# Attention followed by a gated MLP on one core: steps of VectorE and ScalarE in another order, low terms last, short scores read straight through

## The chip, the core and the metric

The kernel runs on one core of a Trainium2 chip. A time is the device time of one execution in microseconds (us), from the first to the last instruction and a little around it. Five engines work side by side, each through its own instructions in order: TensorE (PE, with its weight loads listed apart as PEld), VectorE (DVE), ScalarE (ACT), GpSimd (POOL) and SyncE (SP), which issues nearly all DMAs.

## The reference

```
scores = q @ k^T / sqrt(64) - log(448)          # 8 batches x 12 heads, 448 tokens, head size 64
x      = sigmoid(scores) @ v                    # heads side by side: 448 x 768
h      = relu(x @ w_in)                         # 768 -> 1024
u, v2  = h[:, :512], h[:, 512:]
v_n    = (v2 - mean(v2)) / sqrt(var(v2) + 1e-6) # over the 512 features
v_s    = w_spatial @ v_n + b_spatial            # over the 448 tokens
out    = (u * v_s) @ w_out                      # 512 -> 768
```

All inputs and the output are fp32.

## The kernel before, in words

**Number format.** Most products are made from pairs: a value is rounded to fp32r (the high part), what is lost is kept as a second fp32r (the low part), and three products are added in PSUM: high by high, low by high, high by low (`TERMS`, line 347). So each operand costs a rounding copy (mostly on ScalarE) and a subtraction (on VectorE) before TensorE can use it. A few products run in plain fp32 without a split: the short scores (line 373) and attention times v (lines 440 and 1462).

**Rounds.** The batches are taken in four rounds of two (`m` = 0 to 3). A round has these stages, one after the other on TensorE:

- attention, heads in groups of four. 448 tokens of keys are three full tiles of 128 and a short one of 64. The short tiles of two head pairs share one call of `score_products` with `t == NFULL`: four matmuls on 64 x 64 quarters of the array, in two passes each, so eight matmul records. There are six such calls in a round. Every score product reads the queries through `halves`, which turns the order (t s) into (s t): consecutive columns lie half a row apart. ScalarE applies the sigmoid out of PSUM (`sigmoid`, line 355).
- the v half of the MLP's input: in round 0 plain products and the layer norm by `gate_values`, in rounds 1 to 3 `values_by_blocks`;
- the u half: in round 0 `gated`, in rounds 1 to 3 the first part of `gated_by_blocks`;
- the product over tokens, `spatial` (line 1012), four groups of two PSUM banks, of which the token tiles are the result of the layer norm (`vns`);
- the output product, `output_by_blocks`.

**Seven products for eight.** The block stages (line 1078, `by_blocks`) multiply a 2 x 2 grid of blocks with seven block products. They need sums of operands, made at run time by VectorE: from the four gated blocks (g11, g12, g21, g22) come t1 to t4, each of which has to be rounded (`high`, ScalarE, line 1159) and subtracted (`low`, VectorE, line 1163). The order of the blocks is fixed (`ORDER_1`, `ORDER_V`). The results are accumulated in banks px, pw and py; between blocks ScalarE copies them out (lines 735, 1239, 1325, 1336) and VectorE adds them (lines 738, 1246, 1337, 1353), and a bank can take its next block only after that. Two such banks share one tile.

**What sets the order.** Each engine runs its instructions in program order (`in_program_order`), so the place of a step in the source is its place in the queue. Steps that are not needed at once are generators in `jobs`; `spare(n)` runs the next n pieces of them, and is called from `then` after each block's bank. `rest` (in `values_by_blocks`), `steps` (in `by_tokens`, the layer norm of rounds 1 to 3) and `first_rest` (the sums and splits of the gated blocks) are such jobs. `load_weights(n)` runs n pieces of another generator, which in round 0 decodes and splits the weights w_in and w_out (two pieces for a weight tile, on VectorE and ScalarE, lines 157 to 163 and 252 to 289); `load_weights(99)` before the third `gated` runs all that is left. `high_of_sum` and `low_of_sum` (lines 626 and 630) split the sums of w_out in round 0, and the second sends the result out by a DMA on SP.

In `gate_values` of round 0, ScalarE applies the relu, VectorE the statistics, GpSimd the power of -1/2, and VectorE subtracts the mean (line 799), scales (line 810) and makes the low part (line 811). In `by_tokens`, ScalarE already does the subtraction and the scaling (lines 909 and 911).

Of the kernel before, what the change touches and what calls it, by code (L numbers as in the profile page):

```python
# [35 lines left out]
def attn_gmlp_kernel(  # L36
# [319 lines left out]

    def copied(b, hp, t):
        return t == NFULL - 2
# [7 lines left out]
    def score_products(b, hp, t):  # L366
        psc = banks(f"psc_{b}_{hp}_{t}")
        if t == NFULL:
            for odd in range(2):
                raw = loaded[b, hp + odd]  # L370
                for j in range(2):
# [4 lines left out]
                        halves(raw[rows, HALF + Q :]),  # L376
# [42 lines left out]
    def attention_scores(b, hp, t):  # L419
        psc = score_products(b, hp, t)  # L420
        at = room(b, hp, t)
        if copied(b, hp, t):
            nc.vector.tensor_copy(at, psc)
            subtract_lows()
        else:
            sigmoid(at, psc)
# [221 lines left out]
    def values_by_blocks(m):  # L648
# [24 lines left out]
        def high(name, src):  # L673
            if name == "t1":
                nc.scalar.copy(x1[0], src)
            else:
                for ks, t in to[name]:
# [12 lines left out]
        high("t3", w3)  # L690
# [3 lines left out]
        low("t3", w3)  # L694

        def rest():
            high("t2", w00)
# [72 lines left out]
    def gate_values(ts):  # L770
# [14 lines left out]
        if n > 1:  # L785
            load_weights(1 if ts[0] else 5)
# [10 lines left out]
        nc.gpsimd.tensor_tensor(rstd[:, :n], rstd[:, :n], mhalf[:, :n], op=ALU.pow)  # L797
        for i in range(n):
            nc.vector.tensor_scalar_sub(rv[:, i], rv[:, i], mv[:, i, 0:1])
        load_weights(n - 1)  # L800
        for i, t in enumerate(ts):
            vn = slots["tile"][:, t]
            if t != NFULL:
                parts = [(vn[:, 0], vn[:, 1], slice(0, P))]
            else:

                a, c = slice(0, HALF), slice(HALF, P)
                parts = [(vn[a, 0], vn[c, 0], a), (vn[c, 1], vn[a, 1], c)]
            for hi, lo, rows in parts:
                nc.vector.tensor_scalar_mul(hi, rv[rows, i], rstd[rows, i : i + 1])  # L810
                nc.vector.scalar_tensor_tensor(
                    lo,
                    rv[rows, i],
                    rstd[rows, i : i + 1],
                    hi.bitcast(F32),
                    op0=ALU.mult,
                    op1=ALU.subtract,
                )
            vns[t] = vn
        if n == 1:  # L820
            load_weights(1)

    def by_tokens(m):
# [107 lines left out]
        def steps():  # L931
# [9 lines left out]
            moments(a)  # L941
            relu(b)
            yield True
            relu(c)
# [12 lines left out]
            yield True  # L957
            moments(b)
            yield True
# [38 lines left out]
    def spatial(b, fcs):  # L998
# [3 lines left out]
        for i, fc in enumerate(fcs):  # L1002
            fs = slice(fc * P, (fc + 1) * P)
            ops = [
                (vns[c + 4 if b % 2 else c][:, a, fs], w_sp_s[:, c, p, cols])
# [747 lines left out]
```

## Time and profile before

| | |
|---|---|
| median of 3 runs | 624.38 us (622.73 to 627.30) |
| the profiled execution's own time | 624.51 us |
| its span, first to last instruction | 622.5 us |
| mean granted clock of TensorE in it | 0.999 of full speed |
| busy: PE, PEld | 612.6 us (98%), 487.1 us (78%) |
| busy: DVE, ACT, POOL | 453.4 us (73%), 341.0 us (55%), 21.4 us (3%) |
| DMA | 139.22 MB, 224 GB/s mean |

How to read it: a matmul's record lasts longer than the time until the next one can start, because matmuls are pipelined. So a PE that is busy for 98% is not a PE without waits, and the weight loads (PEld), of which there is one for each matmul, show the waits better: in a stage of 128 x 128 tiles they stand back to back when nothing is late. In the attention stages four loads of 64 x 64 run side by side and PEld is idle most of the time without any wait.

### The profile page before, as it was taken

How to read it: one execution, taken by the hardware profiler on the slowest of the kernel's cores; microseconds unless marked ns; L12 is line 12 of the kernel's file. 1: busy time of each engine (PE TensorE's matmuls, PEld its weight loads, DVE VectorE, ACT ScalarE, POOL GpSimd, SP SyncE). 2: the span in 40 equal slices, each digit the busy share in tenths (PEclk: the TensorE clock that was granted, in tenths of full speed). 3: DMA queues.
4: the chain of work that ended last, by engine and by line, in shares of the span. 5: the costliest groups of instructions: out<-in, count | busy, mean ns of one | idle time of the engine just before them, and what ended most of it. 6: DMA issues, size and time to landing. Idle time of an engine off the chain costs nothing.

```text
span 622.5 us, 10390 instructions
## 1 busy us (share of the span) xinstructions
PE 612.6 (98%) x4136; PEld 487.1 (78%) x4136; DVE 453.4 (73%) x639; ACT 341.0 (55%) x444; POOL 21.4 (3%) x63
## 2 busy tenths in 40 slices
PE   9999999998999999999999999999999999999997
PEld 3556689997856669999984568998996655999996
DVE  4898798999789878278785657628788555935873
ACT  6889313235488863272556785137347766515443
POOL 0000011000000000020000000002000000002000
PEclk9999999999999999999999999999999999999999
DMA  8774853369987879890695652597169554559145
GB/s 291 261 232 143 258 148 105 118 236 325 319 341 282 324 285 327 245 412 11 202 317 204 231 233 102 137 297 300 51 218 368 182 179 189 160 142 380 63 150 179
DMA packets 59632, 139.22 MB, mean 224 GB/s; under 512 B 15680, under 2 KB 31552, under 8 KB 59328
## 3 DMA queue, kind: packets, MB, share of 16 engines
q1 hardware_dynamic: 59152, 138.22, 64.3%
q8 instruction: 32, 0.52, 0.4%
q10 hardware_dynamic: 432, 0.34, 0.2%
q14 instruction: 16, 0.13, 0.1%
HBM read 102.37 MB, written 36.18 MB: 223 GB/s over the span
## 4 chain that ended last, share of the span: by engine, by line
PE 65%; DVE 19%; ACT 8%; DMA 3%; issue 3%; SPq 0%; POOL 0%; ACTq 0%; DVEq 0%
PE pav L1462 14%; PE psc L391 13%; PE vx L1078 7%; PE pg L1012 5%; PE pav L440 5%; PE ux L1078 4%; PE o L1078 4%; PE psc L373 4%; PE vy L1078 3%; PE uy L1078 3%; DVE x_s L1163 3%; ACT x_s L1159 2%; ACT ats L355 1%; PE pv L473 1%; DVE wval_s L160 1%
## 5 line engine op out<-in xcount | busy, mean ns | idle before, releaser
L355 ACT ACTIVATE ats<-psc,fixed 128x896 f32<-128x896 f32 x102 | 95.0, 1015 | 18.0 <-PE pav L1462 10.1
L391 PEld LDWEIGHTS psc<-qks 64*128 64x128 f32 x840 | 77.3, 187 | 14.9 <-issue 7.2
L391 PE MATMUL psc<-qks 64*128 64x448 f32 x840 | 85.4, 359 | 0.0
L1462 PE MATMUL pav<-ats,v 64*64 64x448 f32 x720 | 76.4, 540 | 0.0
L1078 PE MATMUL o<-x_s,w_out 128*128 128x448 f32 x324 | 65.0, 356 | 0.9
L1078 PEld LDWEIGHTS o<-x_s,w_out 128*128 128x128 f32 x324 | 60.0, 189 | 4.9 <-DVE vr L1337 2.6
L1012 PE MATMUL pg<-w_sp_s,mlp 128*128 128x448 f32 x320 | 63.3, 355 | 0.5 <-DVE mlp L916 0.3
L1012 PEld LDWEIGHTS pg<-w_sp_s,mlp 128*128 128x128 f32 x320 | 59.6, 189 | 3.3 <-DVE mlp L916 1.8
L1462 PEld LDWEIGHTS pav<-ats,v 64*64 64x64 f32 x720 | 28.4, 132 | 38.5 <-issue 26.6
L341 DVE TENSOR_TENSOR qks<-raw,qks 128x848 fp32r<-128x848 f32 x46 | 47.3, 1038 | 1.0
L1078 PE MATMUL vx<-x_s,w_g 128*128 128x448 f32 x216 | 43.0, 355 | 0.8 <-ACT vr L735 0.8
L1078 PEld LDWEIGHTS vx<-x_s,w_g 128*128 128x128 f32 x216 | 40.3, 189 | 4.0 <-issue 2.1
L1078 PE MATMUL ux<-x_s,w_u 128*128 128x448 f32 x162 | 32.1, 352 | 0.0
L1078 PEld LDWEIGHTS ux<-x_s,w_u 128*128 128x128 f32 x162 | 30.6, 189 | 0.0
L473 PE MATMUL pv<-w_g_s,x_s 128*128 128x512 f32 x126 | 28.9, 390 | 0.0
L473 PEld LDWEIGHTS pv<-w_g_s,x_s 128*128 128x128 f32 x126 | 23.6, 188 | 5.6 <-PE pav L440 0.7
L473 PE MATMUL pu<-x_s,w_u_s 128*128 128x448 f32 x144 | 27.4, 352 | 0.0
L473 PEld LDWEIGHTS pu<-x_s,w_u_s 128*128 128x128 f32 x144 | 27.2, 189 | 0.0
L440 PE MATMUL pav<-ats,v 128*64 128x448 f32 (+1 forms) x144 | 27.1, 544 | 0.0
L1462 PE MATMUL pav<-at,v 64*64 64x448 f32 x168 | 26.9, 536 | 0.0
L373 PE MATMUL psc<-raw 64*64 64x448 f32 x192 | 26.8, 637 | 0.0
L1246 DVE TENSOR_TENSOR us<-uy,us 128x448 f32<-128x448 f32 x6 | 3.7, 621 | 30.0 <-ACT us L1245 30.0
(205 smaller groups left out, 1003.7 us busy)
## 6 DMA issues: line engine op xcount, KB each, us to landing
raw<-qk_dram SPq DMA_DIRECT2D x47, 456.0 KB, 6.1
w_g<-w_g SPq DMA_DIRECT2D x21, 768.0 KB, 6.2
w_u<-w_u SPq DMA_DIRECT2D x21, 768.0 KB, 7.1
w_out<-w_out SPq DMA_DIRECT2D x21, 768.0 KB, 10.4
v<-v_dram SPq DMA_DIRECT2D x24, 448.0 KB, 4.2
wraw<-w_in_dram SPq DMA_DIRECT2D x12, 512.0 KB, 5.1
v<-vt SPq DMA_DIRECT2D x48, 112.0 KB, 2.6
wraw<-w_out_dram SPq DMA_DIRECT2D x6, 512.0 KB, 4.2
```

Of the source, the lines that this page charges most:

```text
L160: nc.vector.scalar_tensor_tensor(l, a, 3, l, op0=ALU.logical_shift_left, op1=ALU.bitwise_or)
L341: nc.vector.tensor_sub(s[:, 1], loaded[b, hp][:, HALF:], s[:, 0].bitcast(F32))
L355: nc.scalar.activation(at, src, AF.Sigmoid, bias=bias_s, scale=QK)
L373: nc.tensor.matmul(psc[odd * HALF : (odd + 1) * HALF, j, :S], raw[rows, :HALF], halves(raw[rows, HALF + Q :]), start=True, stop=True,)
L391: nc.tensor.matmul(psc[:, j, :S], st[rows, k : k + P], halves(mv[rows, Q:PART]), start=i == 0, stop=i == len(ops) - 1,)
L440: nc.tensor.matmul(pav[heads, odd, :S], vt[rows, t, heads], at[rows, j], start=start, stop=t == NFULL,)
L473: nc.tensor.matmul(ps, st, mv, start=i == 0, stop=i == len(ops) - 1)
L1012: nc.tensor.matmul(pg[:, i, :S], st, mv, start=n == 0 and not ended, stop=n == len(ops) - 1 and ended,)
L1078: nc.tensor.matmul(out_ps, stationary(w, i, k)[:, a], halves(moving[mv][k][c]), start=(to, i) not in started and n == 0, stop=n == len(ops ...
L1159: nc.scalar.copy(homes[name][0][:, i], src[:, i])
L1163: nc.vector.tensor_sub(lo[:, i], src[:, i], hi[:, i].bitcast(F32))
L1462: ins = nc.tensor.matmul(pavs[pair][heads, i % 2, :S], vt[rows, t if t == NFULL else t + i % 2 * (NFULL + 1), heads], at[rows, j], start=i ...
```

## The change

Six edits, without any change of what is multiplied:

- Short scores (`score_products`): the queries are read straight through, not by halves. The permutation is done by ScalarE instead, whose `short_sigmoid` writes the attention weights two elements apart.
- `gate_values` (round 0): ScalarE subtracts the mean and scales; VectorE negates the mean and keeps the low part. `load_weights` is called with other numbers at other places (12 pieces within the four calls of `gate_values`; before, 11).
- `values_by_blocks`: the second third of t3's rounding and t3's low part go from before the first block into the job `rest`, and the first bank of the first block calls `spare` too.
- `by_tokens`: the statistics (`moments`) of tile groups a and b come one call of `spare` later.
- `spatial` and `by_blocks`: the low terms come last (in `by_blocks`, last among those of a bank; in `spatial`, each bank's ten terms are cut in two parts, and the first part is done for both banks before the second).
- `gated_by_blocks` and `output_by_blocks`: `first_rest` becomes `later_parts`, in which the steps have other places; t1 is written over g12 instead of g22; in round 0 the splits of the sums of w_out move from `of_21` into it, and the low part of g21 into `of_22`; the add for t2 moves into `of_22` in rounds 1 to 3; the bank copies of t3 call `spare` too; and `rooms` takes its buffers in another order. One piece of `spare` in attention moves from the first group of four heads to the second.

```diff
+    def short_sigmoid(at, src):
+        sigmoid(
+            at.rearrange("p j (s t) -> p j t s", t=2),
+            src.rearrange("p j (t s) -> p j t s", t=2),
+        )
...
                         raw[rows, :HALF],
-                        halves(raw[rows, HALF + Q :]),
+                        raw[rows, HALF + Q :],
...
-        high("t3", w3)
+        high("t3", w3, 0)
         nc.vector.tensor_sub(xl[:, 1], pav[:, :, :S], xl[:, 0].bitcast(F32))
         nc.vector.tensor_sub(w01, w01, w00)
         nc.vector.tensor_add(w00, w3, w00)
-        low("t3", w3)
 
         def rest():
+            high("t3", w3, 1)
+            low("t3", w3)
+            yield True
             high("t2", w00)
...
             if mv == "11":
                 nc.scalar.copy(r1[:, i], px[i])
-                spare(i)
+                spare(1)
...
+        mean = scale[:, 1]
+        nc.vector.tensor_scalar_mul(mean[:, :n], mv[:, :n, 0], -1.0)
         for i in range(n):
-            nc.vector.tensor_scalar_sub(rv[:, i], rv[:, i], mv[:, i, 0:1])
-        load_weights(n - 1)
+            nc.scalar.activation(rv[:, i], rv[:, i], AF.Identity, bias=mean[:, i : i + 1])
...
+        for i, hi, _, rows in homes:
+            nc.scalar.activation(hi, rv[rows, i], AF.Identity, scale=rstd[rows, i : i + 1])
+        load_weights(steps[1])
+        for i, hi, lo, rows in homes:
+            nc.vector.scalar_tensor_tensor(
+                lo,
+                rv[rows, i],
...
             relu(a)
             yield True
+            relu(b)
+            yield True
             moments(a)
-            relu(b)
-            yield True
             relu(c)
...
             low_parts(d)
             yield True
+            yield True
             moments(b)
-            yield True
             highs(b)
...
+        highs, lows = ([(c, a, p) for c in range(NFULL) for p in range(2 - a)] for a in range(2))
+        short = [(NFULL, b % 2, 0)]
+        if b % 2:
+            terms = highs[:4] + lows[:2] + short + highs[4:] + lows[2:]
+        else:
+            terms = highs + lows + short
+        n = len(terms) // 2
+        for part in (terms[:n], terms[n:]):
+            for i, fc in enumerate(fcs):
+                for term in part:
...
-            ops = [(a, k, c) for k in range(nk) for a, c in TERMS]
+            ops = [(a, k, c) for part in (TERMS[:2], TERMS[2:]) for k in range(nk) for a, c in part]
...
+            def sub_t1():
+                nc.vector.tensor_sub(g12, g22, g11)
+
+            def sub_t4():
+                nc.vector.tensor_sub(r2, g21, g11)
...
+            if m:
+                steps = {
+                    1: (hi("t3"), lo("t3")),
+                    2: (hi("t2"),),
+                    4: (hi("22"), lo("t2")),
+                    5: (sub_t1, hi("t1"), sub_t4),
+                    6: (lo("t1"),),
+                    9: (lo("22"),),
+                    11: (hi("t4"),),
+                    14: (lo("t4"),),
+                }
+            else:
+                steps = {
+                    1: (low_sum("s3"),),
+                    2: (hi("t3"), lo("t3"), hi("22"), high_sum("s2")),
+                    5: (add_t2, hi("t2"), low_sum("s2"), lo("t2"), high_sum("s1")),
+                    6: (sub_t1, hi("t1"), sub_t4),
+                    7: (low_sum("s1"),),
+                    8: (lo("t1"),),
+                    9: (high_sum("s4"), low_sum("s4")),
+                    10: (lo("22"),),
+                    11: (hi("t4"),),
+                    14: (lo("t4"),),
+                }
+            for n in range(15):
+                for step in steps.get(n, ()):
+                    step()
+                yield True
...
         def of_21(pu):
             if not m:
                 high_of_sum("s3")
-                high_of_sum("s2")
             gate(g21, pu)
             high("21", g21)
-            if not m:
-                low_of_sum("s3")
-            low("21", g21)
-            if not m:
-                high_of_sum("s1")
-                high_of_sum("s4")
+            if m:
+                low("21", g21)
 
         def of_22(pu):
             gate(g22, pu)
+            if not m:
+                low("21", g21)
             nc.vector.tensor_sub(g12, g22, g12)
+            if m:
+                add_t2()
...
-                for name in ("c12", "r2", "thirds")
+                for name in ("r2", "c12", "thirds")
...
-            sigmoid(at, score_products(*units[n], NFULL))
+            short_sigmoid(at, score_products(*units[n], NFULL))
...
-                spare(8 if n + 4 == end else 4 if n > first else 5)
+                spare(8 if n + 4 == end else 5 if n > first else 4)
...
+                ((0, 1), (6, 1, 0)),
+                ((2, 3), (1, 1, 0)),
+                ((4, 5), (1, 1, 0)),
+                ((6,), (0, 0, 1)),
```

## Rows read from the trace of the kernel before

**Rows 1.** Windows: length, busy time (instructions) of five engines, clock, DMA share, GB/s.

```profile
66.90:100.00 33.10, 33.10 (x151) 27.71 (x151) 27.18 (x54) 10.21 (x15) 3.48 (x6) 1.00 0.58 174
...
317.70:377.30 59.60, 59.60 (x601) 34.84 (x602) 35.44 (x41) 44.00 (x48) 1.24 (x9) 1.00 0.62 228
```

**Rows 2.** Timeline of PEld, round 2: start, length, form, count, idle before and releaser.

```profile
377.17 3.32 PEld L1078 LDWEIGHTS vx<-x_s,w_g 128*128 128x128 f32 x18 [0.70 <-issue]
381.10 3.32 PEld L1078 LDWEIGHTS vx<-x_s,w_g 128*128 128x128 f32 x18 [0.61 <-ACT vr L735]
...
401.45 3.40 PEld L1078 LDWEIGHTS ux<-x_s,w_u 128*128 128x128 f32 x18
...
415.64 3.33 PEld L1078 LDWEIGHTS uy<-x_s,w_u 128*128 128x128 f32 x18 [0.57 <-DVE stats L886]
...
425.77 1.41 PEld L1012 LDWEIGHTS pg<-w_sp_s,mlp 128*128 128x128 f32 x7
427.79 0.30 PEld L1012 LDWEIGHTS pg<-w_sp_s,mlp 128*128 128x128 f32 x2 [0.60 <-DVE mlp L916]
428.57 2.00 PEld L1012 LDWEIGHTS pg<-w_sp_s,mlp 128*128 128x128 f32 x11 [0.48 <-DVE mlp L916]
...
443.65 6.83 PEld L1078 LDWEIGHTS o<-x_s,w_out 128*128 128x128 f32 x36
...
452.18 2.19 PEld L1078 LDWEIGHTS o<-x_s,w_out 128*128 128x128 f32 x12 [0.48 <-DVE vr L1353]
...
461.58 1.05 PEld L1078 LDWEIGHTS o<-x_s,w_out 128*128 128x128 f32 x6 [0.40 <-DVE vr L1337]
...
468.99 0.21 PEld L373 LDWEIGHTS psc<-raw 64*64 64x64 f32 x8 [0.28 <-issue]
```

**Rows 3.** Timeline of PEld, the output stage of round 0.

```profile
139.13 3.40 PEld L1078 LDWEIGHTS o<-mlp,w_out_s 128*128 128x128 f32 x18
144.24 1.05 PEld L1078 LDWEIGHTS o<-x_s,w_out_s 128*128 128x128 f32 x6 [1.70 <-ACT ur L1325]
...
166.74 0.21 PEld L373 LDWEIGHTS psc<-raw 64*64 64x64 f32 x8 [0.28 <-issue]
```

**Rows 4.** Timeline of all engines, the start of that stage.

```profile
140.12 1.15 DVE L1156 SCALAR_TENSOR_TENSOR g<-pu,g 128x448 f32<-128x448 f32 x2
...
142.20 1.56 ACT L626 CAST w_out_sums<-wt 128x768 fp32r<-128x768 f32 x2
...
143.66 0.52 ACT L1325 COPY ur<-o 128x448 f32<-128x448 f32 x1
```

**Rows 5.** Timeline of all engines, round 2.

```profile
379.21 1.41 ACT L678 CAST xs<-whole 128x896 fp32r<-128x896 f32 x2
...
450.51 1.08 DVE L1174 TENSOR_TENSOR g<-g,g 128x896 f32<-128x896 f32 x1
...
459.07 0.53 ACT L1330 COPY othirds<-o 128x448 f32<-128x448 f32 x1 [1.42 <-PE o L1078]
...
468.27 1.15 DVE L1350 TENSOR_TENSOR or<-o,or 128x448 f32<-128x448 f32 x2
```

**Rows 6.** Groups by line: tile, form, count, then busy us, mean ns, idle before.

```profile
L391 PE MATMUL psc<-qks 64*128 64x448 f32 x840 | 85.4, 359 | 0.0
...
L1462 PE MATMUL pav<-at,v 64*64 64x448 f32 x168 | 26.9, 536 | 0.0
L373 PE MATMUL psc<-raw 64*64 64x448 f32 x192 | 26.8, 637 | 0.0
...
L160 DVE SCALAR_TENSOR_TENSOR wval_s<-wraw,wval_s 128x512 uint32<-128x512 uint32 x18 | 12.4, 688 | 0.2
...
L909 ACT ACTIVATE rv<-rv,scale 128x512 f32<-128x512 f32 x15 | 10.1, 714 | 2.5 <-DVE scale L892 2.4
...
L253 ACT ACTIVATE wraw<-wraw 128x512 f32<-128x512 f32 x12 | 8.3, 692 | 19.1 <-DVE wraw L252 18.8
...
L810 DVE TENSOR_SCALAR mlp<-rv,scale 128x512 fp32r<-128x512 f32 (+1 forms) x8 | 3.8, 481 | 0.8 <-POOL scale L797 0.8
```

More of the change, by code (lines that the diff above doesn't have):

```diff
@@ L671, in values_by_blocks, with high @@
         }
-        def high(name, src):
+        def high(name, src, only=None):
             if name == "t1":
@@ L676, in high @@
             else:
-                for ks, t in to[name]:
+                for ks, t in to[name][only : None if only is None else only + 1]:
                     nc.scalar.copy(t[:, 0], src[:, ks])
@@ L1001, in spatial @@
         pg = pgs[b, fcs]
[L1002 to L1005, printed above, removed]
-                for c in range(NFULL)
-                for a, p in TERMS
-            ]
-            ops.append((vns[NFULL][:, b % 2, fs], w_sp_s[:, NFULL, 0, cols]))
-            ended = (b, fcs) in begun
-            for n, (st, mv) in enumerate(ops):
-                nc.tensor.matmul(
-                    pg[:, i, :S],
-                    st,
-                    mv,
-                    start=n == 0 and not ended,
-                    stop=n == len(ops) - 1 and ended,
-                )
+        ended = (b, fcs) in begun
+        highs, lows = ([(c, a, p) for c in range(NFULL) for p in range(2 - a)] for a in range(2))
[8 more added lines that the diff above has]
+                for term in part:
+                    c, a, p = term
+                    t = c + 4 if b % 2 and c < NFULL else c
+                    nc.tensor.matmul(
+                        pg[:, i, :S],
+                        vns[t][:, a, fc * P : (fc + 1) * P],
+                        w_sp_s[:, c, p, cols],
+                        start=term == terms[0] and not ended,
+                        stop=term == terms[-1] and ended,
+                    )
         begun.add((b, fcs))
@@ L1163, in low, with add_t2 @@
             nc.vector.tensor_sub(lo[:, i], src[:, i], hi[:, i].bitcast(F32))
-        def first_rest():
-            high("22", g22)
-            yield True
-            high("t3", g12)
-            if not m:
-                low_of_sum("s2")
-            low("t3", g12)
-            yield True
-            yield True
-            nc.vector.tensor_add(g11, g12, g11)
-            high("t2", g11)
-            yield True
-            yield True
-            low("t2", g11)
-            low("22", g22)
-            nc.vector.tensor_sub(g22, g22, g11)
-            high("t1", g22)
-            if not m:
-                low_of_sum("s1")
-            low("t1", g22)
-            yield True
-            nc.vector.tensor_sub(r2, g21, g11)
-            if not m:
-                low_of_sum("s4")
-            yield True
-            yield True
-            high("t4", r2)
-            yield True
-            low("t4", r2)
-            yield True
+        def add_t2():
+            nc.vector.tensor_add(g11, g12, g11)
@@ new lines, in later_parts, with hi, lo, high_sum @@
+        def later_parts():
+            sources = {"t3": g12, "t2": g11, "22": g22, "t1": g12, "t4": r2}
+            def sub_t1():
+                nc.vector.tensor_sub(g12, g22, g11)
+            def sub_t4():
+                nc.vector.tensor_sub(r2, g21, g11)
+            def hi(name):
+                return lambda: high(name, sources[name])
+            def lo(name):
+                return lambda: low(name, sources[name])
+            def high_sum(name):
+                return lambda: high_of_sum(name)
+            def low_sum(name):
+                return lambda: low_of_sum(name)
+            if m:
[26 more added lines that the diff above has]
+                yield True
@@ L1325, in then @@
                 nc.scalar.copy(r1[i], px[i])
+                spare(1)
+            elif mv == "t3":
                 spare(1)
```

49 lines of the change are left out of this document (22 added, 27 removed).

## The prediction, as it was put on record

> **What bounds the kernel now.** First the page's busy shares and the windows. In round 2's attention TensorE is busy for all of 59.60 us, ScalarE for 44.00 and VectorE for 35.44 [rows 1]: TensorE sets the pace there, and only cheaper matmuls can help. The block stages I read from the weight loads, because a matmul's record hides a wait. A load of 128 x 128 that nothing delays takes 6.83 / 36 = 0.19 us (more exactly 0.189, since the stalls repeat to the hundredth) [rows 2]. So 126 matmuls, which each of the three block stages of a round has, need 23.8 us. In round 2 the v half starts at 377.17, the u half at 401.45, the token product at 425.77, the output at 443.65 and the next attention at 468.99 [rows 2]. That makes 24.28, 24.32 and 25.34 us for the three stages (from the last I take the 0.28 us of its change of tile): losses of 0.45, 0.5 and 1.25 us. Rounds 1 and 3 show the same waits within 0.2 us. Round 0's output stage runs from 139.13 to 166.74 [rows 3]: 27.61 − 0.28 − 23.8 = 3.5 us lost. These losses, and the short scores, are what the change can reach; each wait names a copy or an add that stood behind other work in its queue.
>
> **The change, part by part**
>
> *Short scores.* All three products here have 448 columns. The fp32r one, read by halves, has records of 359 ns; the plain fp32 one of short scores, read by halves, 637; the plain fp32 one by v, read straight, 536 [rows 6]. The last two have the same tile shape and differ by 101 ns. There are 192 records, four side by side, so 48 passes: 48 × 0.101 = 4.8 us if the reading is the reason. The means hold stretched records too, so I take 0.093 a pass, 4.5 us. Ends: 0 (the two tiles differ in more than the stride) and 4.8. All but the first calls of a round lie on TensorE's path. ScalarE now writes two elements apart. The nearest row reads and writes two apart in place: 692 ns for 512 elements, against 714 for 512 plain ones [rows 6]. I take nothing; the upper end is a doubling, 1 us a call, six a round, against 59.6 − 44.0 = 15.6 us in which ScalarE is free [rows 1].
>
> *Round 0's layer norm.* VectorE loses 15 passes of about 481 ns, ScalarE gains 15 of 714 [rows 6], and four small negations come. By the Trainium skill, "ScalarE: Activation LUTs", Rules for kernel authors, such adds and multiplies belong on VectorE; the sum would then lose 15 × 0.23 = 3.5 us. The rows of the window say otherwise: ScalarE is busy for 10.21 of 33.10 us, VectorE for 27.18 [rows 1], so I put ScalarE's time at nothing. VectorE's saving is not worth 7 us either: its low parts now wait for GpSimd's power and ScalarE's copies, and by stepping the four groups forward the last low part ends where it did. What is left is one piece of weight work that moves into VectorE's idle time, two joins of 0.69 [rows 6]: everything queued on VectorE from there to the output stage comes 1.4 us earlier. SP's load of the next weight tile moves with it.
>
> *Round 0's output.* Before, VectorE reaches g21's gate at 140.12, ScalarE casts two sums of w_out at 142.20 and only then copies the first bank, 143.66 to 144.18 [rows 4], on which TensorE waits until 144.24 [rows 3]. After: gate at 138.7, rounded by 140.8; first bank's copy by 141.4, before TensorE wants the second block at 139.13 + 18 × 0.189 = 142.5. VectorE then does g22's gate, g21's low part and the difference (about 1.1 each) until 143.3, a sum's low part and t3's until 145.3, and the three adds by 146.9; TensorE wants the first of these banks at 145.9. The sums that follow stay ahead by a few tenths, except t1's low part, which I put 0.3 late. SP's write of the first sum falls behind the raw loads, of which no user is near. So 3.5 becomes about 0.4: **3.1 us**. Ends: 1.5 (VectorE not earlier) and 3.5.
>
> *Values, rounds 1 to 3.* ScalarE rounds t3 twice, 1.41 us, before the first bank's copy, and TensorE waits [rows 5, 2]. One rounding (about 0.47) now stands behind that copy: 0.45 becomes 0.1, times three **1.1**. t3's low part comes later, but low terms last give it 1.1 us.
>
> *u half.* The wait of 0.57 us is for an add behind the statistics of group a [rows 2]. They now follow it: 3 × 0.5 = **1.5**. The statistics are then 0.6 late for the token product, which wants them: next item.
>
> *Token product.* Round 2 waits 0.60 and 0.48 us for low parts [rows 2]. Low terms last gives those two microseconds, but the fifth term is now a high part of the third tile, which I find about 0.8 late there, for its data come by DMA. Rounds 1 and 3 hardly wait. **0.5** in all; ends −0.5 and 1.5.
>
> *Output, rounds 1 to 3.* The third block waits 0.48 us for an add behind t2's sum, 450.51 to 451.59; the copy of t2's third bank waits until 459.07 for a buffer, which delays the next copies, and the sixth block waits 0.40 and 0.48 [rows 2, 5]. The sum now stands before the stage, and the buffer is free early. New: a copy of the first block stands behind t3's rounding, 0.3, and t2's sum pushes the adds by 0.1. 1.25 becomes 0.4: **2.5**. Against it: before, the last add ends 469.42 (468.27 + 1.15) [rows 5], as TensorE is done. VectorE does as many passes as before, so a shorter output leaves its adds behind, and the next attention's second bank waits: −0.3 for each of three starts, with 0.1 of each faster short call lost: **−1.0**.
>
> The piece of `spare` that moves in attention, and the relus that move by a step, lie under TensorE's work; uncovered they would cost their 1 us each.
>
> Sum: 4.5 + 3.1 + 1.1 + 1.5 + 0.5 + 2.5 − 1.0 = 12.2 us. The profiled execution took 624.51 us, 0.13 over the median, so the sum goes on either: 624.5 − 12.2 = **612.3 us**.
>
> **Rivals**
>
> 1. *The short reads give nothing.* For: the fp32r product is read by halves as well and shows no penalty, 359 ns [rows 6]. Against: 637 and 536 for like tiles. The Trainium skill, "TensorE: Matmul & The Clock Gate", Part 2, Step-by-step, says of the fill that the time depends on the number of columns alone; by that rule the reading would be free either way. The two fp32 groups of the trace, with equal columns, disagree with it. Time: 612.3 + 4.5 = 616.8. Chance 0.12.
> 2. *VectorE becomes the bound round the output stages.* What the reordering takes out of the waits there comes back as waits for its adds and for the statistics, because its work is the same. For: it runs from 140 us on without a pause, and its last adds end with TensorE. Against: the waits of before come from order, not from load. If half of the non-short gains (7.7) go: 616.2. Chance 0.18.
> 3. *Slower: ScalarE's strided write.* Place: the short sigmoid of every call. Free time is 15.6 us a round [rows 1], six calls: past 2.6 us more per call, ScalarE would be the bound of the attention, and past about 3.3 it would eat the 12 us in three rounds. At 4 us more, 3 × (24 − 15.6) = 25 us against 12: 638. Nothing in the rows is near it. Chance 0.03.
> 4. *More than forecast.* All waits named go: 3.5 + 1.35 + 1.5 + 1.1 + 3.7 + 4.8 = 16.0, 608.5. Chance 0.09.
>
> **How the numbers follow.** The forecast holds 0.58. The range 608.0 to 618.0 takes in rivals 1, 2 and 4 with the ends of the terms, and leaves out the slower case and a mixture of 1 and 2 (620), together near 0.15. 1% is about what a measurement of this kernel can tell from no change; faster by more than that means under 618.1: 0.58 + 0.09 + most of 0.12 and 0.18, say 0.85. Within 1%: 0.12, where rivals 1 and 2 meet. Slower: 0.03.
>
> **What would show it.** Short scores: records near 540 ns, and attention stages about 1.1 us shorter in each round. Output of round 0: no load waiting more than 0.5 us, and g21's gate within a microsecond of the start of the stage. Rounds 1 to 3: v half and u half within 0.2 us of 23.8, no wait on line 1353 or 1337 over 0.2, and a new small one at the output's second block or at the next attention's start. Wrong would be: short records still at 630; the short sigmoid far over 1 us; new waits on VectorE that add up to more than 2 us a round.

## The result, and the profile after

The changed kernel takes 614.02 us (median of 613.41 to 615.16) against 624.65 for the kernel before on the same chip: a ratio of **0.983**, interval 0.981 to 0.985. That is 10.6 us less; forecast were 12.2 (612.3 us, range 608 to 618). The execution with a profile is the longest of its four, 615.16 us with a span of 613.4, so the stages below add up to 9.1 us, the difference of the two spans, and not to 10.6.

A stage is measured from the first weight load of one to that of the next, as in the prediction; the output of round 3, behind which nothing comes, to the end of its last weight load. Gains in us, rounds 1 to 3 together unless a round is named:

| Stage | before | after | gain | forecast |
|---|---|---|---|---|
| attention, four rounds (62.87, 59.85, 59.59, 59.37 before) | 241.68 | 237.17 | 4.5 | 4.5 − 1.0 |
| round 0, from its v half to the end of its u half | 72.35 | 72.29 | 0.1 | 0 |
| round 0, output | 27.61 | 24.62 | 3.0 | 3.1 |
| v half | 72.85 | 71.49 | 1.4 | 1.1 |
| u half | 73.16 | 73.09 | 0.1 | 1.5 |
| token product | 51.02 | 51.66 | −0.6 | 0.5 |
| output | 75.72 | 74.99 | 0.7 | 2.5 |

Both rows of round 0 and the v half came as forecast. The attention gave what was forecast for the short scores, without the −1.0; 0.8 of its 4.5 us lie in the first attention, which varies by a microsecond from kernel to kernel. The last three rows should have given 4.5 and gave 0.2.

Windows of the changed kernel, in answer to [rows 1]:

```profile
66.12:99.22 33.10, 33.10 (x152) 27.72 (x153) 25.06 (x49) 19.07 (x29) 3.36 (x6) 1.00 0.65 206
311.24:369.60 58.36, 58.36 (x601) 34.50 (x602) 36.28 (x42) 44.20 (x48) 1.26 (x9) 1.00 0.63 232
```

In round 0's layer norm ScalarE went from 10.21 to 19.07 us, VectorE from 27.18 to 25.06. Round 2's attention is 1.2 us shorter at the same work. Groups by line, in answer to [rows 6]:

```profile
L397 PE MATMUL psc<-qks 64*128 64x448 f32 x840 | 84.8, 356 | 0.0
...
L1500 PE MATMUL pav<-at,v 64*64 64x448 f32 x168 | 26.9, 536 | 0.0
...
L379 PE MATMUL psc<-raw 64*64 64x448 f32 x192 | 22.0, 543 | 0.0
...
L355 ACT ACTIVATE at<-psc,fixed 128x896 f32<-128x896 f32 x12 | 13.2, 1102 | 3.0 <-PE psc L379 3.0
```

The short score product is now as cheap as the product by v (543 against 536 ns; before, 637). The short sigmoid takes 1102 ns; the plain ones average 1017. Weight loads of round 0's output and round 2, in answer to [rows 3] and [rows 2]:

```profile
138.29 3.40 PEld L1093 LDWEIGHTS o<-mlp,w_out_s 128*128 128x128 f32 x18
141.69 3.40 PEld L1093 LDWEIGHTS o<-x_s,w_out_s 128*128 128x128 f32 x18
145.28 3.32 PEld L1093 LDWEIGHTS o<-x_s,w_out_sums 128*128 128x128 f32 x18 [0.18 <-ACT w_out_sums L634]
...
153.25 5.97 PEld L1093 LDWEIGHTS o<-mlp,w_out_sums 128*128 128x128 f32 x32 [0.49 <-DVE mlp L1178]
...
369.48 3.32 PEld L1093 LDWEIGHTS vx<-x_s,w_g 128*128 128x128 f32 x18 [0.70 <-issue]
372.96 3.32 PEld L1093 LDWEIGHTS vx<-x_s,w_g 128*128 128x128 f32 x18
...
393.31 3.40 PEld L1093 LDWEIGHTS ux<-x_s,w_u 128*128 128x128 f32 x18
...
407.88 3.32 PEld L1093 LDWEIGHTS uy<-x_s,w_u 128*128 128x128 f32 x18 [0.95 <-issue]
...
414.88 3.32 PEld L1093 LDWEIGHTS uy<-x,w_u 128*128 128x128 f32 x18 [0.27 <-DVE scale L904]
418.21 0.76 PEld L1027 LDWEIGHTS pg<-w_sp_s,mlp 128*128 128x128 f32 x4
419.76 2.95 PEld L1027 LDWEIGHTS pg<-w_sp_s,mlp 128*128 128x128 f32 x16 [0.80 <-ACT mlp L923]
...
426.81 0.30 PEld L1027 LDWEIGHTS pg<-w_sp_s,mlp 128*128 128x128 f32 x2 [0.42 <-ACT mlp L923]
427.60 8.62 PEld L1027 LDWEIGHTS pg<-w_sp_s,mlp 128*128 128x128 f32 x46 [0.49 <-DVE mlp L928]
...
436.22 5.67 PEld L1093 LDWEIGHTS o<-x_s,w_out 128*128 128x128 f32 x30
442.83 1.05 PEld L1093 LDWEIGHTS o<-x_s,w_out 128*128 128x128 f32 x6 [0.93 <-ACT wval_s L1361]
444.09 3.32 PEld L1093 LDWEIGHTS o<-x_s,w_out 128*128 128x128 f32 x18 [0.20 <-DVE vr L1391]
```

The wait of 1.70 us in round 0's output is gone, and so is that of 0.61 in the v half, now 23.83 us long in each round, which is 126 loads back to back. In the output of round 2 the waits of [rows 2] are gone too, but a new one of 0.93 stands at the second block, and the same in rounds 1 and 3 (0.94 each). The token product has new waits, 0.42 and 0.49, for the parts of tile group b; the 0.49 is there in every round. The wait of 0.80 at its fifth load in round 2 is the one that the prediction had put there.

All engines of the changed kernel, in answer to [rows 4] (the gate, then the copy of the first bank):

```profile
136.78 1.15 DVE L1171 SCALAR_TENSOR_TENSOR g<-pu,g 128x448 f32<-128x448 f32 x2
...
139.81 0.54 ACT L1361 COPY ur<-o 128x448 f32<-128x448 f32 x1 [0.85 <-PE o L1093]
...
144.25 0.82 ACT L634 CAST w_out_sums<-wt 128x768 fp32r<-128x768 f32 x1
```

and, in answer to [rows 5], VectorE and ScalarE round the start of round 2's output stage (436.22):

```profile
427.46 1.08 DVE L1048 TENSOR_TENSOR g<-pg,b_bc 128x896 f32<-128x896 f32 x1
...
430.68 1.09 DVE L1178 TENSOR_TENSOR x_s<-g,x_s 128x896 fp32r<-128x896 f32 x1 [1.00 <-ACT x_s L1174]
...
440.28 1.09 DVE L1253 TENSOR_TENSOR g<-wval_s,g 128x896 f32<-128x896 f32 x1
441.41 0.94 ACT L1174 CAST x_s<-g 128x896 fp32r<-128x896 f32 x1 [2.00 <-DVE g L1253]
442.25 0.53 ACT L1361 COPY wval_s<-o 128x448 f32<-128x448 f32 x1
```

This is the place to read slowly. The copy of the third bank (442.25) stands in ScalarE's queue behind the rounding of t3 (441.41), which waits for the difference on VectorE (440.28 to 441.37). TensorE wanted that bank at 436.22 + 30 × 0.189 = 441.89. The difference is the end of a chain of VectorE that begins with the bias of g11 at 427.46 and takes 13.9 us. So two remedies offer themselves: take the copy out from behind the rounding, or make the chain end earlier. The experiments try both.

### The profile page after: what moved, and what is told of

It reads as the page before. It is cut to its first block, busy times and chain, and to the rows that moved or that the text cites. A ratio compares the mean times of both kernels' runs of the same rounds, so it can differ in the third digit from the quotient of the medians.

```text
span 613.4 us, 10394 instructions
## 1 busy us (share of the span) xinstructions
PE 604.1 (98%) x4136; PEld 486.3 (79%) x4136; DVE 447.5 (73%) x628; ACT 353.0 (58%) x459; POOL 24.3 (4%) x63
## 4 chain that ended last, share of the span: by engine, by line
PE 75%; DVE 9%; ACT 8%; DMA 3%; issue 2%; SPq 1%; POOL 1%; POOLq 0%; DVEq 0%; ACTq 0%
PE pav L1500 16%; PE psc L397 13%; PE o L1093 11%; PE vx L1093 8%; PE pv L481 5%; PE pav L448 4%; PE pu L481 4%; PE ux L1093 3%; PE vy L1093 3%; PE psc L379 3%; ACT mlp L923 3%; PE pg L1027 2%; DVE g L1171 2%; DVE g L1048 2%; ACT x_s L1174 2%
## 5 line engine op out<-in xcount | busy, mean ns | idle before, releaser
L1093 PE MATMUL o<-x_s,w_out 128*128 128x448 f32 x324 | 63.4, 354 | 1.8 <-ACT wval_s L1361 1.8
L1174 ACT CAST x_s<-g 128x896 fp32r<-128x896 f32 x14 | 13.1, 939 | 41.0 <-DVE g L1171 27.0
```

Of the source, the lines that this page charges most:

```text
L1093: nc.tensor.matmul(out_ps, stationary(w, i, k)[:, a], halves(moving[mv][k][c]), start=(to, i) not in started and n == 0, stop=n == len(ops ...
L1174: nc.scalar.copy(homes[name][0][:, i], src[:, i])
```

## The experiments

The stages below are those of the table; a ratio is against the kernel before on the same chip. The first attention and its loads vary by themselves: in the kernels below with the same code it took 61.3 to 62.3 us. So the whole is read from the ratio and a cause from its stage.

**1. Short scores alone, on the kernel before.**

```
...
-                        halves(raw[rows, HALF + Q :]),
+                        raw[rows, HALF + Q :],
...
-            sigmoid(at, score_products(*units[n], NFULL))
+            short_sigmoid(at, score_products(*units[n], NFULL))
```

> The kernel before with the short scores' edit alone (queries read straight through, ScalarE writes two apart). Theory (the plain fp32 product pays for the stride of its reading, 0.093 us a pass): short records from 637 to about 540 ns, attention of rounds 1 to 3 from 59.85, 59.59 and 59.37 to about 58.4 us each, the whole 4.5 us shorter, about 620.0 us. Rival (the attention stages became shorter because VectorE's adds end earlier, or the records differ for another reason): records or stages stay within 0.3 us of the kernel before, the whole within 1 us of it.

620.2 us, ratio 0.994 (0.992 to 0.996), 3.9 us. Records of 542 ns, attention of rounds 1 to 3 at 58.73, 58.63 and 59.04; v half, u half and output as before to 0.2. So the reading is the reason for the dearer records. The stages of rounds 1 to 3 give 2.4 us by this edit alone where 3.6 were expected, and the rest of the 3.9 lies in the first attention, which varies. 0.3 to 0.7 us of each start remain, for which the trace shows a wait for raw loads; the changed kernel, at 58.36, does not have them.

**2. The old order of the statistics.**

```
-            relu(b)
-            yield True
             moments(a)
+            relu(b)
+            yield True
             relu(c)
...
-            yield True
             moments(b)
+            yield True
             highs(b)
```

> The changed kernel with the old order of the statistics in the layer norm of rounds 1 to 3 (a and b one call earlier). Theory (the late statistics of b, not the low terms, cause the new waits of 0.42 and 0.49 us of the token product): the token product of rounds 1 and 3 shrinks from 16.87 and 16.78 to about 16.1, the u half grows from 24.06 and 24.13 to about 24.5; the whole within 1 us of the changed kernel. Rival (the fifth term, a high part of the third tile, causes them): token product unchanged, u half 0.4 longer each, the whole 1.2 us longer.

610.15 us, ratio 0.977 (0.975 to 0.979): some 4 us less than the changed kernel, which neither theory had. Token products 16.28, 16.67 and 16.28; u half 24.32, with the wait of 0.56 us of before; and the output stages, in which nothing was edited, fell from 25.09 to 24.11, that is to 126 loads and the 0.28 of the change of tile. In round 2 VectorE's chain begins 433.16 − 423.35 = 9.81 us ahead of the output stage (in the changed kernel, 436.22 − 427.46 = 8.76), and the stage's loads run on without a wait:

```profile
423.35 1.09 DVE L1048 TENSOR_TENSOR g<-pg,b_bc 128x896 f32<-128x896 f32 x1
...
433.16 10.21 PEld L1093 LDWEIGHTS o<-x_s,w_out 128*128 128x128 f32 x54
```

The edit of the statistics, for which the prediction had entered a gain, costs more than it brings, and most of it in a stage two further on.

**3. Round 0's layer norm as before**, with its weight pieces at the old places (the functions of the kernel before put back).

> The changed kernel with round 0's layer norm as before (VectorE subtracts the mean and scales, the weight pieces at the old places). Theory (VectorE being earlier carries half of the gain of round 0's output stage): g21's gate begins 1 us after the start of the output stage instead of 1.5 us before it, and the stage goes from 24.62 to 26.1 us or more; the whole 1.5 us or more longer. Rival (the order of ScalarE's casts and copies carries it alone): the stage at most 0.3 us longer.

615.47 us, ratio 0.985 (0.983 to 0.988). The gate of g21 begins 1.01 us after the output stage does (before, 0.99), and the stage takes 25.70 us. So of the 3.0 us gained there 1.9 come from the order of the casts and copies, and 1.1 from VectorE being earlier. The gate moved as the theory had it, but the stage stayed under the theory's 26.1 and well over the rival's 0.3: both have a share. The prediction's lower end for the term, with VectorE not earlier, was 1.5. The whole holds something else too: the attention of round 1 took 59.55 us here (58.36 in the changed kernel), with a wait of 1.01 for raw loads at its start.

**4. Bank adds first.**

```
-                    1: (hi("t3"), lo("t3")),
-                    2: (hi("t2"),),
-                    4: (hi("22"), lo("t2")),
-                    5: (sub_t1, hi("t1"), sub_t4),
+                    2: (hi("t3"),),
+                    4: (lo("t3"), add_t2, hi("t2")),
+                    5: (hi("22"), lo("t2"), sub_t1, hi("t1"), sub_t4),
...
             nc.vector.tensor_sub(g12, g22, g12)
-            if m:
-                add_t2()
```

> The changed kernel, but in the output stages of rounds 1 to 3 the rounding of t3 follows the third bank's copy, and t3's low part and the sum for t2 follow the first bank adds. Theory (the wait of 0.94 us at the second block comes only from the copy's place behind the rounding of t3): that wait goes, the stages fall from 25.09 to about 24.3 us each, the whole about 2 us shorter than the changed kernel. Rival (VectorE's load is the bound there): the 0.94 us come back as waits for VectorE's adds or low parts at the third or fourth block, the whole within 0.7 us of the changed kernel.

611.45 us, ratio 0.979 (0.977 to 0.982); output stages 24.30, 24.29 and 24.02. The copy no longer waits; 0.24 us are left at the third block, for t3's low part. The first remedy works.

**5. Statistics of b early, those of a late.**

```
             highs(a)
+            moments(b)
             low_parts(d)
             yield True
             yield True
-            moments(b)
             highs(b)
```

> The changed kernel with one step moved: in the layer norm of rounds 1 to 3 the statistics of b come ahead of d's low parts, where VectorE waits 1.35 us for ScalarE anyway; a's statistics stay late. Theory (b's statistics behind the last adds make b's parts late, and with them every VectorE step up to the output stage): the waits of 0.42 and 0.49 us go, the token products fall to about 16.1 to 16.3 us, and the output stages fall from 25.09 to about 24.1 us without any edit there; u half at 23.83 where the loads come in time; the whole 5 us or more shorter than the changed kernel, about 608 us. Rival (the output stage's 0.94 us are its own, from the copy behind t3's rounding): the token product falls as above, the output stages stay at 25.09; about 612 us.

610.79 us, ratio 0.979 (0.977 to 0.981). Token products 16.43, 16.45 and 16.29, close to what the theory expected. The output stages only fell to 24.97, 24.98 and 24.33, in rounds 1 and 2 nearer to the rival: TensorE leaves the token product earlier, but VectorE's chain still begins behind b's last low part, in round 2 at 424.25:

```profile
424.25 1.08 DVE L1048 TENSOR_TENSOR g<-pg,b_bc 128x896 f32<-128x896 f32 x1
...
433.12 5.67 PEld L1093 LDWEIGHTS o<-x_s,w_out 128*128 128x128 f32 x30
439.62 1.05 PEld L1093 LDWEIGHTS o<-x_s,w_out 128*128 128x128 f32 x6 [0.82 <-ACT wval_s L1361]
```

That is 8.87 us ahead of the output stage in rounds 1 and 2 and 9.24 in round 3, where the stage lost less; the kernel of experiment 2 has 9.8 to 10.2, the changed kernel 8.76 in every round. What counts for the output is that distance, not the token product's length. How much of what is left comes from a's statistics, which stay late here, was not separated.

**6. The token product's terms in the old order.**

```
-        for part in (terms[:n], terms[n:]):
-            for i, fc in enumerate(fcs):
-                for term in part:
...
+        for i, fc in enumerate(fcs):
...
+            ops = [
+                (vns[c + 4 if b % 2 else c][:, a, fs], w_sp_s[:, c, p, cols])
+                for c in range(NFULL)
+                for a, p in TERMS
+            ]
```

> The changed kernel with the token product's terms in the old order (high, low, high tile by tile; bank after bank). Theory (low terms last gives the low parts about a microsecond): waits for low parts come earlier, the token products about 0.5 us longer each, and nothing comes back later; the whole 1 to 2 us longer than the changed kernel. Rival (the waits are for b's parts and come up in either order): token products within 0.2 us.

615.12 us, ratio 0.986 (0.984 to 0.987). The whole is as expected, but not its parts: the token products are 1.0 to 1.5 us longer each (18.41, 19.01, 18.32), two to three times the forecast, and the output stages 1.0 shorter (24.11, 24.12, 23.83): TensorE waits earlier, and VectorE's chain has the time. "Nothing comes back later" was wrong. It is the clearest view of the trade: of the 4.1 us that low terms last saves in the token products, 2.9 are paid back in the outputs, as long as the chain is late. The rows show how. In the changed kernel TensorE itself waits for b's last low part (427.60 above) and then has 46 loads left, 46 × 0.189 = 8.7 us, until the output stage. VectorE's chain begins right behind that same low part (427.46), so it cannot have more than about that time. In the kernel before, with the low terms in their old places, TensorE waited for the layer norm's last low parts with 53 loads left:

```profile
433.57 1.08 DVE L1033 TENSOR_TENSOR g<-pg,b_bc 128x896 f32<-128x896 f32 x1
433.71 9.95 PEld L1012 LDWEIGHTS pg<-w_sp_s,mlp 128*128 128x128 f32 x53 [0.35 <-DVE mlp L916]
```

The chain began 443.65 − 433.57 = 10.08 us ahead of the output, and in experiment 6 it does so again, 10.08 in every round. Low terms last puts the wait seven loads, 1.3 us, nearer to the output, and the chain loses that time.

**7. VectorE scales, weight pieces at the new places.**

```
-        mean = scale[:, 1]
-        nc.vector.tensor_scalar_mul(mean[:, :n], mv[:, :n, 0], -1.0)
...
-            nc.scalar.activation(rv[:, i], rv[:, i], AF.Identity, bias=mean[:, i : i + 1])
+            nc.vector.tensor_scalar_sub(rv[:, i], rv[:, i], mv[:, i, 0:1])
...
-            nc.scalar.activation(hi, rv[rows, i], AF.Identity, scale=rstd[rows, i : i + 1])
+            nc.vector.tensor_scalar_mul(hi, rv[rows, i], rstd[rows, i : i + 1])
```

> The changed kernel, but in round 0's layer norm VectorE subtracts the mean and scales, as before; the weight pieces stay at their new places. Theory (of the 2.5 us by which VectorE is earlier, 1.4 come from the moved weight piece and the rest from the work given to ScalarE): g21's gate between 0.5 us before and the start of the output stage, the stage at about 25.0 us (24.62 with both, 25.70 with neither). Rival (the passes taken from VectorE carry it all): gate 1 us after the start, 25.7 us. Other rival (the place of the pieces carries it all): 24.6 us.

619.33 us, ratio 0.993 (0.991 to 0.995): 5 us longer than the changed kernel. None of the three had that. The output stage is at 24.63, as the other rival said, but this run cannot tell the three apart: round 0's token product takes 22.78 us instead of 16.54, and with TensorE 6 us late g21's gate (139.97) begins 3.7 us ahead of the output stage (143.68). Weight loads of this kernel, and its windows:

```profile
101.84 0.50 PEld L997 LDWEIGHTS pg<-w_sp_s,mlp 64*128 64x128 f32 x3 [3.60 <-ACT rv L797]
102.88 13.56 PEld L1025 LDWEIGHTS pg<-w_sp_s,mlp 128*128 128x128 f32 x60 [0.54 <-issue]
```

```profile
100.00:102.00 2.00, 0.16 (x2) 0.16 (x2) 1.97 (x5) 1.15 (x2) 0.00 (x0) 0.69 0.01 4
102.00:104.00 2.00, 2.00 (x6) 1.38 (x7) 1.76 (x4) 0.00 (x0) 0.52 (x2) 0.50 0.00 0
104.00:106.00 2.00, 2.00 (x6) 1.81 (x6) 1.36 (x3) 0.00 (x0) 0.57 (x1) 0.50 0.00 0
106.00:108.00 2.00, 2.00 (x8) 1.82 (x7) 1.93 (x5) 0.62 (x1) 0.00 (x0) 0.61 0.00 0
108.00:110.00 2.00, 2.00 (x12) 2.00 (x11) 1.97 (x5) 0.74 (x2) 0.00 (x0) 1.00 0.99 264
```

The new places put six weight pieces ahead of the first group's norm. With VectorE scaling as well, the chain of the four groups ends late. ScalarE's relu of the last tile (101.22; 98.58 in the changed kernel) stands behind a step of a weight piece that waits for that chain, and the weight loads stand still for 3.60 us for the bank. Then its granted clock (third number from the end) is 0.50, half of full speed, until past 106 us, and the 60 loads take 13.56 us instead of 11.3. So of the 6.2 us, 3.9 are waits and 2.3 the slower loads behind them. The new places pay only because ScalarE takes the passes. The fourth combination, ScalarE's passes with the pieces at their old places, was not run, so what the passes are worth alone is not shown.

**8. Block products' terms in the old order.**

```
-            ops = [(a, k, c) for part in (TERMS[:2], TERMS[2:]) for k in range(nk) for a, c in part]
+            ops = [(a, k, c) for k in range(nk) for a, c in TERMS]
```

> The changed kernel with the block products' terms in the old order (high by high, low by high, high by low for each tile in turn, in place of the last kind at the end of a bank). Theory (low terms last gives each low part 4 to 6 loads more, 0.6 to 0.8 us): the v half, in which t3's low part now comes later, loses about 0.4 us a round, the output stages about 0.5; the whole 2 to 3 us longer than the changed kernel. Rival (the low parts are early enough in either order): the whole within 0.7 us.

615.44 us, ratio 0.986 (0.985 to 0.988). The v halves lose 0.26 us each, round 0's output 0.37, the outputs of rounds 1 to 3 nothing: 1.2 us by stages, between the two expectations.

**9. One low part later, nothing else.** The changed kernel's chain holds two idle spells of 1.00 us in which VectorE waits for ScalarE's rounding (one is at 430.68 above). The first is filled:

```
             gate(g11, pu)
             high("11", g11)
-            low("11", g11)
+            if not m:
+                low("11", g11)
 
         def of_12(pu):
             gate(g12, pu)
+            if m:
+                low("11", g11)
```

> The changed kernel with one step of VectorE moved in rounds 1 to 3: the low part of g11, for which VectorE waits 1.00 us idle each time (it needs ScalarE's rounding), comes behind the gate of g12. Nothing is added or taken away. Theory (the waits at the output's second block come from VectorE being one microsecond late at the head of its chain of gates, 13.9 us long in every kernel so far): the chain is 1 us shorter, the difference for t3 ends 4.2 us after the start of the stage instead of 5.2, the 0.94 and 0.20 us go nearly, output stages from 25.09 to about 24.2; the whole 2.5 us shorter than the changed kernel. Rival (the order of the copy and t3's rounding alone decides): the 0.94 us stay within 0.2, output stages at 24.9 or more.

611.69 us, ratio 0.981 (0.979 to 0.982). The output stages are 24.11, 24.11 and 23.84 (round 3 has no change of tile behind it): no loss at all. Weight loads, VectorE and ScalarE of this kernel, round 2:

```profile
425.35 1.08 DVE L1048 TENSOR_TENSOR g<-pg,b_bc 128x896 f32<-128x896 f32 x1
...
434.11 7.07 PEld L1093 LDWEIGHTS o<-x_s,w_out 128*128 128x128 f32 x37
...
437.18 1.09 DVE L1256 TENSOR_TENSOR g<-wval_s,g 128x896 f32<-128x896 f32 x1
438.31 0.94 ACT L1174 CAST x_s<-g 128x896 fp32r<-128x896 f32 x1 [1.01 <-DVE g L1256]
...
439.15 0.53 ACT L1364 COPY wval_s<-o 128x448 f32<-128x448 f32 x1
```

The copy still stands behind the rounding. But the chain is 12.9 us long, the difference ends 4.16 us after the stage's start (5.15 in the changed kernel), and the bank is copied at 439.68, before TensorE wants it at 434.11 + 5.67 = 439.78. So the second remedy works alone too, with the same number of passes on VectorE.

**10. Experiments 5 and 9 together.**

> The changed kernel with both one-step moves: b's statistics ahead of d's low parts, and g11's low part behind the gate of g12. Theory (the waits add up along one chain of VectorE, and both moves shorten it): token products 16.3 to 16.5 us, output stages about 24.2, u half 23.83 where loads come in time; about 607.5 us. Rival (a wait that goes comes back elsewhere): the sum of token product and output stage stays over 41.0 us in rounds 1 and 2.

608.82 us (expected, 607.5), ratio 0.976 (0.974 to 0.977). Token products 16.29, 16.73 and 16.29, output stages 24.11, 24.11 and 23.84, u half 23.83 to 23.84, v half 23.82 to 23.83. Token product and output together take 40.40 and 40.84 us in rounds 1 and 2, under the rival's 41.0: nothing came back.

**11. Experiment 4's move on top.**

> The changed kernel with three moves in rounds 1 to 3: b's statistics ahead of d's low parts, g11's low part behind the gate of g12, and in the output stage the bank adds ahead of t3's low part and the sum for t2. Theory: with VectorE a microsecond earlier the 0.24 us that were left at the third block go as well, output stages 23.9 to 24.1 us, token products 16.3 to 16.5, u half 23.83; about 607 us, no slower than the changed kernel with the old order of the statistics (610.15). Rival: the third move adds nothing to the two others, or costs a few tenths at t2.

609.82 us, ratio 0.977 (0.976 to 0.979); output stages 24.29, 24.30 and 24.03. The rival holds: the third move brings nothing to the other two and leaves its own 0.24 us at the third block.

**12. The short sigmoid's other side, on the kernel of experiment 10.**

```
-            at.rearrange("p j (s t) -> p j t s", t=2),
-            src.rearrange("p j (t s) -> p j t s", t=2),
+            at.rearrange("p j (s t) -> p j s t", t=2),
+            src.rearrange("p j (t s) -> p j s t", t=2),
```

> As the changed kernel with b's statistics ahead of d's low parts and g11's low part behind the gate of g12 (608.8 us), and the short sigmoid takes its other way round the same reordering: ScalarE reads the scores out of PSUM half a row apart and writes straight on. Theory (the 0.09 us that a short sigmoid takes longer than before, 1102 against 1008 ns, are the price of writing two apart, and lie off TensorE's path): the short sigmoids fall to about 1010 ns, the whole within 1 us of 608.8. Rival (reordering costs ScalarE the same from either side): they stay near 1100.

608.31 us, ratio **0.975** (0.973 to 0.977), the same as experiment 10 within the interval, and well under both kernels of this case. Groups by line of this kernel:

```profile
L355 ACT ACTIVATE at<-psc,fixed 128x896 f32<-128x896 f32 x12 | 12.1, 1009 | 3.0 <-PE psc L379 3.0
```

1009 ns, against 1102 when it writes two apart and 1008 in the kernel before: the price was the writing, and it lay off TensorE's path, as far as the interval can tell.

## Why the prediction was right, and where it was not

The time lies in the range and 1.7 us over the forecast. That it came so near is in part luck: the token product and the output of rounds 1 to 3, forecast at 3.0 us together, gave 0.1 in the profiled execution, and a third of that miss is hidden by the −1.0 for the attention starts, which was not needed. By its steps:

- **Short scores** (4.5): right. Records at 543 ns, attention of rounds 1 to 3 1.2 us shorter each (forecast, 1.1), and the whole 3.9 (2.7 to 5.3) by the edit alone. Rival 1 falls. The Trainium skill's sentence that the fill depends on the columns alone ("TensorE: Matmul & The Clock Gate", Part 2, Step-by-step) does not hold for the plain fp32 product here: 633 and 536 ns medians at 448 columns, by the reading alone. The Trainium skill's "Advanced Engine Details and Errata", Memory Cachelines, says that SBUF is read in lines of 16 bytes and that changing the line at each access costs; it gives no price. Here the plain fp32 product pays 97 ns of 633; the fp32r product, read by the same halves, shows none (356 to 359 ns), and the block products, fp32r by halves, have the same 352 ns median as the token product, fp32r read straight, with tiles of the same shape.
- **Round 0's layer norm**: the result was right and half of the reasoning wrong. ScalarE's time did cost nothing. But VectorE was 2.5 us earlier at the output, not 1.4, and "VectorE's saving is not worth 7 us" because the low parts would wait missed what the passes are for: without them the new places of the weight pieces cost 6.2 us in round 0's token product (experiment 7). The rule of the Trainium skill that I weighed ("ScalarE: Activation LUTs", Rules for kernel authors) would have kept them on VectorE; here the engine with time to spare decides, and not the faster one.
- **Round 0's output** (3.1): right, 3.0, for the reasons given, with the split of experiment 3. The gate was further ahead than thought, 1.51 us before the start of the stage where the prediction had 0.4. What is left is t1's low part, 0.49 late where I had 0.3 (the load at 153.25), and 0.18 for the cast of a sum.
- **Values** (1.1): right, 1.4. Low terms last is part of it: without it 0.26 a round is lost again (experiment 8).
- **u half** (1.5): the mechanism is right and this execution hides it. In experiments 9 and 10 the u half is 23.83 to 23.84 in all rounds, 0.5 under the old order, as forecast. In the changed kernel's profile three things took it back: a wait of 0.95 in round 2 for a block of w_u (its loads stand on SP behind the writes of v, at 401.70), and waits of 0.27 to 0.38 for adds behind statistics that started late after their loads. They vary with the loads: experiment 6 has 24.57 in round 2 with the same code, experiment 4 23.83. In eight of the eleven kernels in which a's statistics follow the adds, the three u halves take 71.5 to 71.7 us together, so the term of 1.5 is there.
- **Token product** (0.5) **and output of rounds 1 to 3** (2.5): here the prediction failed, and it is one step. It said that the statistics are "then 0.6 late for the token product" and let low terms last cover it; and it priced the copy behind t3's rounding at 0.3. It did not carry the lateness on. The layer norm's last low part comes late, TensorE waits for it with 46 loads left where it had 53, and VectorE's chain from the bias of g11 to the difference begins 8.76 us ahead of the output instead of 10.08. Since nothing in the chain, as it stood, has slack, about a microsecond arrives at the second and third block: 0.94 + 0.20 us, in each round. Experiments 2 and 6 show the origin (with the old order of the statistics, or of the terms, no loss in the output), experiments 4 and 9 the path (the copy out of the chain's way: 0.24 left; the chain 1 us shorter: no loss). In one sum the edit of the statistics brings 1.5 in the u half and costs about 2.4 in the token products and 2.9 in the outputs, 3.8 net; experiment 2, without it, is some 4 us shorter.
- **Attention starts** (−1.0): wrong. The wait for the output's last adds is there, 0.67 us at the second bank of round 3's start, but the stages are 58.36 us long with it, within 0.1 of the shortest in any kernel here. The start is not longer than before even with the wait: the first load of a full tile comes 463.10 − 461.31 = 1.79 us after the first load of the stage, in the kernel before 471.04 − 468.99 = 2.05 (rounds 1 and 2: 1.75 and 1.80, before 2.34 and 2.26).

```profile
461.31 0.21 PEld L379 LDWEIGHTS psc<-raw 64*64 64x64 f32 x8 [0.28 <-issue]
462.19 0.21 PEld L379 LDWEIGHTS psc<-raw 64*64 64x64 f32 x8 [0.67 <-DVE or L1388]
463.10 5.03 PEld L397 LDWEIGHTS psc<-qks 64*128 64x128 f32 x54 [0.70 <-DVE or L1388]
```

The same of the kernel before:

```profile
471.04 5.03 PEld L391 LDWEIGHTS psc<-qks 64*128 64x128 f32 x54 [0.90 <-issue]
```

- **Rival 2** (VectorE becomes the bound round the output stages) was in part what happened: of 7.7 us that were not short scores, about 3 did not come in the profiled execution. But its reason, "because its work is the same", is not the cause. Experiment 9 takes no pass away from VectorE and the loss is gone: it was an order with 1 us of waiting inside, not load.

## What to carry to other kernels

A step moved to a later place has to be followed along its engine's queue, stage by stage, until the queue has slack again; the wait that it makes may show two stages on, at another engine's instruction, and the nearest stage may even get shorter. In a chain that sets the time, look for the spells in which the engine waits for its own helper (round, then subtract) and put a step that is ready in between: one such step moved brought the output stages 2.9 us here. And a product that is dear for its reading order can be read straight and reordered by an engine with time to spare.

## What the runs showed of the hardware

- A plain fp32 product (64 x 448) took 633 ns (median) with its moving operand read by halves and 536 read straight. The fp32r products showed no such price: with tiles of 128 x 128 and 448 columns, 352 ns (median) by halves in the block products and 352 read straight in the token product.
- ScalarE wrote 896 fp32 values per partition two apart in 1102 ns, against 1009 straight; to read them out of PSUM half a row apart cost it nothing (1009 against 1008 ns).
- After the wait of 3.60 us in round 0 of experiment 7, TensorE's granted clock was 0.50 (1.2 GHz) from 102 to past 106 us, while it was busy throughout, and 1.00 (2.4 GHz) from 108 on; of the 6.2 us that this token product took longer, 2.3 are the slower loads.
